# Attention into a wave-MLP on one core: three more sets of tiles turned by transposing transfers, and a rewritten order of all steps

## The chip, the core and the metric

The kernel runs on one core of a Trainium2 chip. The metric is the device time of one launch in microseconds (us). TensorE (PE) has its own queue for weight loads (PEld) beside that of the matmuls; VectorE (DVE), ScalarE (ACT), GpSimd (POOL) and SyncE (SP) each run their own instructions in program order and wait for one another through semaphores. All transfers of this kernel, in and out of the chip's memory or from one on-chip tile to another, are issued by SP, one after the other.

## The reference, cut to what matters

```python
# q, k, v: (8 batches, 8 heads, 576 rows, 64), float32; factor = 4
out_d   = softmax(mean4(q) @ mean4(k).T / 8) @ mean4(v)     # 144 rows, repeated 4 times
out_loc = softmax(where(|i-j| < 4, q @ k.T / 8, -1e9)) @ v  # a band of width 7
x = (repeat4(out_d) + out_loc)  as (8, 576, 512)
theta = x @ w_theta
y = w_tok_r @ (x * cos(theta)) + w_tok_i @ (x * sin(theta)) # over the 576 rows
u = x + y
return u + max(u @ w_ch, 0)                                 # (8, 576, 512) float32
```

## The kernel before, in words

Everything is one straight program over 8 batches, with no loop on the chip. Each piece of work is a *step*, a small Python function with a two-letter name, and the text `ORDER` (lines 57 to 98) names the steps one after the other. A step issues its instructions when its word is read, and `pin()` (line 696) ties each instruction to the one before it on its engine, so the text fixes the order of every engine's queue and of SP's. The letters behind a word choose the place: a PSUM bank or pair of banks for TensorE's steps, one of 14 staging tiles for loads, and `v`, `a` or `g` (VectorE, ScalarE, GpSimd) for copies and elementwise work that more than one engine can do. In the kernel before, the steps of one name come in a fixed sequence (batch by batch, line 709), and the word holds only the place.

The steps of one batch, in the order in which the data needs them:

- **Loads and casts.** `lk`, `lq` load two heads of k or q (line 288); `ck`, `cq` cast them to bf16 (line 297). `lv`, `lw` load the two halves of one of five row blocks of v (line 349), `cv` casts them (line 397). Batch 0 takes v another way (`l1`, `c1`, `t1`, `e1`, `x1`, lines 367 to 395).
- **Turning k and q.** `tp` turns two heads pairs on TensorE with 9 transposes (line 304) and `ev` copies the result out (line 317). For batch 7 a transposing transfer does it (`dk`, line 308).
- **Coarse attention.** `kd`, `qd` sum groups of 4 (lines 323, 331 to 337), `pv` and `vd` do it for v, `sd`, `ed`, `nd`, `xn`, `xd`, `xc` are scores, exponentials, weighted sums, normalization, a transpose and its copy.
- **Band attention.** `ps` (line 483) are scores of 116 rows at a time, `ex` exponentials, `mk` the multiplication with the band mask (line 502, on VectorE or GpSimd), `po` the weighted sums (line 512), `nm` the normalization on VectorE (lines 520, 521), `xt` and `xa` turn the result and add the coarse part (lines 531, 537). This gives `xT`, x with the 512 channels on partitions.
- **Wave.** `th` (line 548) is theta, `cs` its cosine and sine on ScalarE (lines 553, 554), `tt`, `ct`, `zt` the same for the last 64 rows. For `zz` (line 594, VectorE), which multiplies x by cosine and sine, x is needed with the rows on partitions: `xm` turns a quarter of it with 4 transposes on TensorE into a PSUM bank (line 587), or `dx` does it with a transposing transfer of SP into the tile `xx` (line 590). `xx` exists once and is shared by all batches that use it; four `dx` fill it, and each of the four `zz` needs all four.
- **Mixing.** `mx` is 9 matmuls (line 610), `ua` adds x on VectorE (line 615) and gives `uT`.
- **Last part.** `ch` is u @ w_ch (line 635). The residual u with rows on partitions, `ur`, comes from `up` (4 transposes on TensorE, line 624) and `uc` (a copy, line 627), or from `du`, a transposing transfer (line 619). `rl` (line 640, VectorE) makes the output tile, `st` stores it. `ut`, `dt`, `ht`, `rt`, `ss`, `sr` do the last 64 rows of two batches at a time.

`xm` serves batches 0 to 5 and `dx` batches 6 and 7; `up` serves batches 0 to 3 and `du` batches 4 to 7. The word `wm` issues matmuls on a tile of zeros whose result is not used (line 715); the text has 37 of them. `te` and `ts` load ScalarE's table for exponentials or for sines (line 720).

Of the kernel before, what the change touches and what calls it, by code (L numbers as in the profile page):

```python
# [8 lines left out]
FP32 = mybir.dt.float32  # L9
# [5 lines left out]
P = 128  # L15
# [14 lines left out]
NCH = 5  # L30
# [15 lines left out]
XDMA = (6, 7)  # L46

RPE = (0, 1, 2, 3)
# [9 lines left out]
l10 l11 c1g c1g k0 l12 lk3 l14 ckg c1v lk5 wm0b t101 c1g e1a kcg wm24 t123 e1a lq6 wm45 x12 cva ckg x13 cva x10 cvv  # L58
cqg lq7 lk8 lk9 tp45 cqg kcg kcg x12 lqa eva lqb kdg cvv kca cka wm62 tp67 lkc x13 lkd cvv eva ckv wm13 pv01 cqv lq0
la2 cqg lb1 tp45 qdv eva wm22 tp23 eva wm65 ps67 kdg vdv lq3 qdv ckg cka ps45 cag ex wm25 sd23 ex lb4 ed cbg lk5 sd01  # L60
cqg ps67 mkv ed po45 nm po23 nd45 nd01 la6 nm la7 xn xn lk8 mkg tp23 cag po45 ex xt6 po01 cqa eva la9 lqa mkg caa xd7
lqb ckg xca ckg nm tp23 nm xt4 xt5 lbd cag lbc cbg lb2 xt7 xa cqg lb1 eva lb0 cbg lb3 lb6 tp01 xa po23 th4 xa xm5 xa
lv7 cqg nm cbg th6 lw xt7 cbg th2 lv5 xm3 evv cbg ts cs tp01 lv8 lv9 cs cbg xa tt4 zz cs xm5 wp6 wp2 zz lw lw wp3 lw
lv4 lw cbg lqa zz ct lqd eva qdg ztv wp7 cba th4 wcv zp5 lkb xm6 wcv lkc kdg wcv wp2 wp3 wcv zcv wp0 wcv wp1 cs wp7
wca wcv ps45 lk2 lk1 wcv wcv ps23 te ex qdg ps01 lq0 zz kdv cva ex mx7 mx6 mx4 cvg ua sd23 cvg cvg mkv lc3 ex po01 ua
sd67 ed ed mkv mx5 ua nm po23 ua po01 cvg pv67 nm nm mkg vda mx4 ua po23 lq6 cqg po67 nd01 nm nd45 mx2 up3 xn lq7 ckg
xn cqg lk5 cka nm tp01 xd4 lk8 up5 uca eva xcv xt3 ucv lk9 tp67 cka xt4 xt0 ua ckg xt1 kdg lv4 xa xa xa mx5 xa eva lva
tp23 ua th4 xt0 lw xa evv cqg th5 xm1 lvb lcd lqc tt0 lw lk1 lv2 lv0 lw ts cs lw xm4 cqg cs tp67 ckg cqg th2 xm3 th5
ct lw cka zz tp01 cs qdg zz cs xm2 evv ztg lc6 lc5 zp4 mx6 ccg zz qdg zcv zz eva cvg mx7 ps45 te ex ua ps23 ua ckg kdv
ex mkv ps01 mx6 lq7 mx7 po45 sd23 ex lq8 lk3 kdg ed cvg sd01 cqg ckg ua lk4 lq9 mx6 tp23 mkv lva lw lvc lw nm ua tp45  # L70
up7 cvg mkv cvv ed mx0 eva cvg pv23 ccg ua ucv eva po67 po45 ua nm up1 nm vda ccg ccg ch0 nd67 lq1 xn nd23 lkb cqg cqa
tp45 uca qdg xn mx1 xd2 xt3 eva ps67 rl lq0 ua po45 xcv kdg qdg ps01 ch2 xa ckg ex mkg nm rl mx3 ps67 cqg lv2 cka po45
ex ua sd01 lkd xt2 ckg ex nm mx3 xt4 xt5 xa up2 ua cqa cqg tp67 cvv ed up3 xa evv uca th0 xa lv6 xt1 up2 xa lw th4 xm6
ucv ts cs uca th5 cvg lq5 ckg po01 cvg zz cs nm po23 xm7 cs ch6 nm tt4 tp01 lw ct tp23 th5 rl mkg ch4 lq7 zz st eva
evv rl po67 sd01 cs cqg cvg ztg po23 ch5 nm nm rl ch4 lv8 lw te ed cvg st pv67 vda zp0 zca lk4 cka lk3 lk1 tp23 cqa
mkg ckg lq9 lqb rl qdg lva lw xm1 eva ckg utg lv0 zz lw xm5 ch4 nd67 lvc zz xn lw nd01 mx5 lvd xn mx6 st ps23 rl lv2
ua po01 kdg nm ps45 ua mx7 lk5 ex xd0 cqa xt1 ex up6 ua xcv ucv lk6 kdv tp23 cqg utg mx0 tp45 qdg xa ua eva sd67 xt2
lv8 xt3 ch1 eva xa mkg ed xa th0 mkv rl cvg lk3 lw xt6 xt7 xa xa lw lk1 cvg th2 mx1 ua ts cs xm3 cvg tt0 zz th6 st lq4
cs cvg cka po45 dt cvg ckg ct po23 th7 mx1 ztg lk7 cs lvb nm pv45 cs ckg po67 cqg kdg lw nm ua sd23 mx0 cvg nm te ed
zp1 tp67 vdv zcv ht2 tp45 xm1 rt lw ua lq9 mx3 eva zz ps67 eva ua lva qdg po45 nm ex ps01 lq0 ex xm2 up3 zz lqc nd67  # L80
uca lvd tp45 cqa xm2 qdg xn nd01 zz mx3 cka cka xn mx2 xd0 up1 lk2 lv6 kdg st ua mx3 cqa mkv lw uca xcv eva tp67 xt0
up1 lk5 ua ua cva ucv xt4 xa mx5 st xa st eva ps23 mkg sd01 qdg po67 lw ed ua nm lv3 xt4 mx5 xt6 cva mx7 po01 ua ex
sd23 xa xa po45 lw nm cvg th6 nm lq4 cqv xt0 lw ed cvv xa ts cs tp23 mkv lv8 th1 cs xm4 ua ch5 kdg lw rl ch6 lv9 eva
tt0 th1 th7 xm5 pv23 utv ct ztg zz up0 ss cqg cs zz vdv mx1 uca ua xm0 lv1 lw st zz cs tp45 lv7 cvg lv0 cvg lqb nd23
xm7 ch1 eva kdg rl nd45 xn mx0 rl xn dz ch1 sr ps23 ps45 lw lw qdg lw te ex lka zz po67 ua mx0 ex ps23 cqa ex nm rl ua
lkd ps67 mkv po45 mx1 up0 mkg nm ckg sd23 po45 ua mkg lqc nm ex sd67 utg cka cvg lv6 uca mx1 ch0 cva xt4 ua st st xd1
xca cvg mx5 ed mx1 ed up2 lw xa ua rl xt3 ua uca pv45 cqg po67 xa lq4 nm po01 xt2 cvv th3 up6 vda ucv lq3 xt7 mx4 ch5
# [6 lines left out]
xa th0 zz xa ztg dz tt2 zz zz cs rl mx1 ch4 ct cs ch2 dx dx rl rl dx dx th5 ua mx4 ua cs zz mx2 ua ch4 mx0 zz zz mx1  # L94
ua ua mx2 st mx0 rt ztg cs dz st st ua du zz ua mx5 st ss du ua du mx1 rl ua mx0 ua mx1 mx0 ua ua du st du mx1 mx0 ua
mx1 du ua ua mx0 ch1 ua du rl ch0 ch5 ch1 ch4 rl ch0 ch3 sr du utv rl st st utg dt rl st ch1 rl rl st ht0 rl st rl rt
st st st ss sr
"""


@with_exitstack
def kernel(
# [414 lines left out]
    def nm(b, c, w):  # L517
        ps = at.pop(("po", b, c))
        r = rl[c % 2]
# [238 lines left out]
```

## Time and profile before

| | |
|---|---|
| runs timed | 3: 231.39, 231.49, 232.36 us; median 231.49 |
| profiled execution, first to last instruction | 229.4 us |
| busy: PE, PEld, DVE, ACT, POOL | 219.7, 154.2, 185.6, 159.3, 144.1 us |
| share of the 16 DMA engines | 83.4% |
| transposing transfers | 36 (8 `dx`, 16 `du`, 4 `dz`, 4 `dk`, 4 `dt`) |

The profile has no other time of the profiled execution than its span; the difference to the median of the runs, 2.1 us, is what lies before the first and behind the last instruction of the record. A matmul's busy time is from its start to its modelled end, and matmuls overlap, so a busy PE is not a full one: what one step costs the PE queue is read from the chain of work, where each step stands with the time until the next.

### The profile page before, as it was taken

How to read it: one execution, taken by the hardware profiler on the slowest of the kernel's cores; microseconds unless marked ns; L12 is line 12 of the kernel's file. 1: busy time of each engine (PE TensorE's matmuls, PEld its weight loads, DVE VectorE, ACT ScalarE, POOL GpSimd, SP SyncE). 2: the span in 40 equal slices, each digit the busy share in tenths (PEclk: the TensorE clock that was granted, in tenths of full speed). 3: DMA queues.
4: the chain of work that ended last, by engine and by line, in shares of the span. 5: the costliest groups of instructions: out<-in, count | busy, mean ns of one | idle time of the engine just before them, and what ended most of it. 6: DMA issues, size and time to landing. Idle time of an engine off the chain costs nothing.

```text
span 229.4 us, 8506 instructions
## 1 busy us (share of the span) xinstructions
PE 219.7 (96%) x3491; PEld 154.2 (67%) x3491; DVE 185.6 (81%) x377; ACT 159.3 (69%) x239; POOL 144.1 (63%) x190
## 2 busy tenths in 40 slices
PE   7898899999999999999999999899999999999992
PEld 2455778696778765776788667676676665677740
DVE  5168999999899899797898969979898889476382
ACT  2389899759987899689887896779879258600000
POOL 7768999929999989991984456892697310200000
PEclk9999999999999999999999999999999999999998
DMA  6999999999989999999998007996576357376677
GB/s 181 387 391 391 268 190 222 374 271 226 235 270 249 248 345 177 231 261 233 291 220 211 21 17 191 302 214 126 136 132 187 68 118 206 74 207 160 94 239 241
DMA packets 76647, 49.35 MB, mean 215 GB/s; under 512 B 61120, under 2 KB 61120, under 8 KB 76608
## 3 DMA queue, kind: packets, MB, share of 16 engines
q1 hardware_dynamic: 76608, 48.81, 83.4%
q8 instruction: 27, 0.44, 0.8%
q14 instruction: 12, 0.10, 0.1%
HBM read 33.98 MB, written 9.44 MB: 189 GB/s over the span
## 4 chain that ended last, share of the span: by engine, by line
PE 86%; DVE 7%; DMA 3%; issue 2%; SPq 1%; ACT 0%; POOL 0%; DVEq 0%
PE PS L610 30%; PE PS L548 12%; PE PS L635 12%; PE PS L304 5%; PE PS L531 4%; PE PS L512 3%; DMA st<-in_v_dram 3%; PE PS L587 2%; PE PS L483 2%; PE PS L448 2%; PE PS L560 2%; DVE tmp L521 2%; PE PS L624 2%; PE PS L652 2%; PE PS L453 1%
## 5 line engine op out<-in xcount | busy, mean ns | idle before, releaser
L610 PE MATMUL PS<-WT,z 128*128 128x288 bf16 x576 | 77.9, 286 | 0.2 <-issue 0.2
L610 PEld LDWEIGHTS <-z 128*128 128x128 bf16 x576 | 54.3, 98 | 15.8 <-issue 0.9
L615 DVE TENSOR_TENSOR uT<-PS,xT 128x288 bf16<-128x288 f32 x64 | 28.8, 452 | 11.8 <-PE PS L610 10.9
L548 PE MATMUL PS<-wth,xT 128*128 128x512 bf16 x128 | 32.2, 379 | 0.0
L635 PE MATMUL PS<-wch,uT 128*128 128x512 bf16 x128 | 31.1, 379 | 0.0
L569 POOL TENSOR_TENSOR zT<-xT,cst 128x512 bf16<-128x512 bf16 x7 | 8.1, 1153 | 34.0 <-ACT cst L566 34.0
L521 DVE TENSOR_TENSOR tmp<-PS,rl 128x512 bf16<-128x512 f32 x40 | 27.7, 692 | 1.4
L502 POOL TENSOR_TENSOR pm<-pm,band 128x1024 bf16<-128x1024 bf16 (+1 forms) x14 | 25.0, 1789 | 4.5 <-ACT pm L491 4.5
L537 DVE TENSOR_TENSOR xT<-PS,xdT 128x464 bf16<-128x464 f32 (+1 forms) x40 | 24.0, 629 | 3.0 <-ACT xdT L471 2.0
L640 DVE SCALAR_TENSOR_TENSOR osb<-PS,ur 128x512 f32<-128x512 f32 x32 | 21.8, 685 | 4.7 <-PE PS L635 4.2
L491 ACT ACTIVATE pm<-PS 128x1024 bf16<-128x1024 f32 (+1 forms) x24 | 20.4, 879 | 6.5 <-PE PS L483 6.5
L553 ACT ACTIVATE cs<-PS,pihc 128x512 bf16<-128x512 f32 x32 | 22.2, 693 | 1.6 <-PE PS L548 1.4
L720 ACT ACT_TABLE_LOAD x15 | 19.2, 1283 | 0.3
L331 POOL TENSOR_TENSOR two<-kT 128x580 f32<-128x580 bf16 x13 | 15.0, 1152 | 7.0 <-ACT kT L317 5.3
L635 PEld LDWEIGHTS <-uT 128*128 128x128 bf16 x128 | 11.9, 98 | 11.1
L554 ACT ACTIVATE cs<-PS 128x512 bf16<-128x512 f32 x32 | 19.2, 601 | 0.0
L594 DVE TENSOR_TENSOR z<-PS,cs 128x1024 bf16<-128x1024 bf16 x24 | 16.0, 682 | 2.3 <-PE PS L587 1.8
L548 PEld LDWEIGHTS <-xT 128*128 128x128 bf16 x128 | 11.3, 98 | 9.6 <-DVE xT L537 0.2
L331 POOL TENSOR_TENSOR two<-qT 128x576 f32<-128x576 bf16 x13 | 14.9, 1145 | 4.3 <-ACT qT L317 4.0
L438 ACT ACTIVATE pd<-PS 128x864 bf16<-128x864 f32 x16 | 13.8, 888 | 5.0 <-PE PS L427 4.9
L397 POOL CAST v_w<-st 128x512 bf16<-128x512 f32 x26 | 16.8, 672 | 0.0
L317 ACT COPY qT<-PS 128x1152 bf16<-128x1152 bf16 x13 | 14.6, 1121 | 2.0 <-PE PS L304 2.0
(116 smaller groups left out, 427.0 us busy)
## 6 DMA issues: line engine op xcount, KB each, us to landing
st<-in_k_dram SPq DMA_DIRECT2D x32, 288.0 KB, 6.0
st<-in_q_dram SPq DMA_DIRECT2D x32, 288.0 KB, 6.1
st<-in_v_dram SPq DMA_DIRECT2D x70, 128.0 KB, 5.2
out_dram<-osb SPq DMA_DIRECT2D x32, 256.0 KB, 2.4
st<-in_v_dram SPq DMA_DIRECT2D x4, 288.0 KB, 3.2
st<-in_moe_w_tok_r_dram SPq DMA_DIRECT2D x4, 288.0 KB, 6.5
st<-in_moe_w_tok_i_dram SPq DMA_DIRECT2D x4, 288.0 KB, 7.4
st<-in_moe_w_theta_dram SPq DMA_DIRECT2D x4, 256.0 KB, 6.3
```

Source lines behind the costliest of these rows:

```text
L331: nc.gpsimd.tensor_tensor(out=t, in0=src[:, :, 0:2], in1=src[:, :, 2:4], op=ALU.add)
L491: nc.scalar.activation(out=pm[(3 * b + u) % NPM][:, :, 0:n].rearrange("p e c j w -> p e (c j w)"), in_=at.pop(("ps", b, u))[:, :, 0:4 * W ...
L502: EW[w].tensor_tensor(out=t, in0=t, in1=m, op=ALU.mult)
L521: nc.vector.tensor_tensor(out=tmp[(NCH * b + c) % NTMP].rearrange("p g (j d) -> p g j d", d=D), in0=ps[:, :, :, 0:D], in1=r.unsqueeze(3).t ...
L537: nc.vector.tensor_tensor(out=xT[b % 2][:, :, CH * c:CH * c + cnt].rearrange("p e (m j) -> p e m j", j=4), in0=at.pop(("xt", b, c))[:, :, ...
L548: nc.tensor.matmul(out=ps, lhsT=xT[b % 2][:, dc, P * c:P * c + P], rhs=wth[:, dc, :], start=(dc == 0), stop=(dc == 3))
L553: nc.scalar.activation(out=t[:, 0, :], in_=ps, func=AF.Sin, bias=pihc, scale=1.0)
L554: nc.scalar.activation(out=t[:, 1, :], in_=ps, func=AF.Sin, bias=0.0, scale=1.0)
L610: nc.tensor.matmul(out=ps, lhsT=z[b % 2][:, j, P * dc:P * dc + P], rhs=WT[:, j, cols], start=(j == 0), stop=(j == 8))
L615: nc.vector.tensor_tensor(out=uT[b % 2][:, dc, cols], in0=at.pop(("mx", b, i)), in1=xT[b % 2][:, dc, cols], op=ALU.add)
L635: nc.tensor.matmul(out=ps, lhsT=uT[b % 2][:, dc, P * c:P * c + P], rhs=wch[:, dc, :], start=(dc == 0), stop=(dc == 3))
L640: nc.vector.scalar_tensor_tensor(out=o, in0=at.pop(("ch", b, c)), scalar=0.0, in1=ur[b % 2][:, c, :], op0=ALU.max, op1=ALU.add)
```

## The change

The two constants that choose the way of `x` and of the residual change, the scratch tile of `nm` gets five copies in place of two, each word of the order now names its step in full (name, batch, part, then the place behind a dot), so that steps of one name may come in any sequence, and the whole text of the order is new, with other places and engines.

```diff
-XDMA = (6, 7)
+XDMA = (4, 5, 6, 7)
-RPE = (0, 1, 2, 3)
+RPE = (0, 1, 2)
 ORDER = """
-l10 l11 c1g c1g k0 l12 lk3 l14 ckg c1v lk5 wm0b t101 c1g e1a kcg wm24 t123 e1a lq6 wm45 x12 cva ckg x13 cva x10 cvv
-cqg lq7 lk8 lk9 tp45 cqg kcg kcg x12 lqa eva lqb kdg cvv kca cka wm62 tp67 lkc x13 lkd cvv eva ckv wm13 pv01 cqv lq0
...
-mx1 du ua ua mx0 ch1 ua du rl ch0 ch5 ch1 ch4 rl ch0 ch3 sr du utv rl st st utg dt rl st ch1 rl rl st ht0 rl st rl rt
-st st st ss sr
+l100.0 c100.g kc1.a kc2.g l103.1 c103.a l102.2 c102.a wm.27 t101.01 e101.v kc0.a l101.3 lq01.4 lq00.5 cq00.v c101.g
+wm.42 t100.23 e100.a cq01.g wm.42 tp001.01 lk03.6 ck03.g lq03.7 lq02.8 kc3.a lk02.9 cq02.g ck02.g x104.2 cq03.v cv04.v
...
+xt71.4 du53 nm72.v th60.5 vd7.a nd70.23 th62.6 cs62.a xn70.v dx61 nd71.01 xn71.v st43 xt73.2 th63.3 xt72.6 xd7.7 st31
...
+ua74.v du72 mx72.2 ua73.v ua72.v du71 mx71.0 ch61.1 ua71.v ut7.v mx70.0 ch63.4 dt3 rl61.v st61 ua70.v ch62.5 du70
+rl63.v st63 rl62.v st62 ch60.0 rl60.v ch72.4 rl72.v ht3.5 rt3.v sr2 st60 st72 ss3 sr3 ch70.0 rl70.v st70 ch73.4 ch71.5
+rl73.v st73 rl71.v st71
 """
-    rl = tiles(2, [P, 2, 4], "rl", FP32)
+    rl = tiles(NCH, [P, 2, 4], "rl", FP32)
-        r = rl[c % 2]
+        r = rl[c]
-    todo = {kind: iter(seq) for kind, (_, seq) in STEPS.items()}
+    todo = {(kind,) + tuple(args) for kind, (_, seq) in STEPS.items() for args in seq}
     for word in ORDER.split():
-        kind, place = word[:2], word[2:]
+        word, _, place = word.partition(".")
+        kind, args = word[:2], tuple(int(x) for x in word[2:])
...
-        STEPS[kind][0](*next(todo[kind]), place)
+        todo.remove((kind,) + args)
+        STEPS[kind][0](*args, place)
```

The new text has 20 `wm` matmuls in place of 37, 16 `dx` in place of 8 and 20 `du` in place of 16, 16 `xm` in place of 24 and 12 `up` in place of 16. Steps that several engines can do, as VectorE / ScalarE / GpSimd:

| step | before | after |
|---|---|---|
| casts of k and q (`ck`, `cq`) | 3 / 20 / 41 | 9 / 11 / 44 |
| v blocks (`cv`) | 7 / 7 / 26 | 8 / 13 / 19 |
| w_tok (`cb`) and their turned copies (`wc`) | 8 / 2 / 8 | 10 / 4 / 4 |
| w_theta, w_ch (`ca`, `cc`) | 0 / 1 / 7 | 1 / 1 / 6 |
| `ev` and `e1` | 5 / 27 / 2 | 7 / 25 / 2 |
| sums of four (`kd`, `qd`) | 6 / 0 / 26 | 6 / 0 / 26 |
| masks (`mk`) | 10 / 0 / 14 | 11 / 0 / 13 |
| `uc`, `xc`, `vd`, `zc` | 17 / 19 / 0 | 13 / 19 / 0 |
| `zt`, `ut` | 5 / 0 / 11 | 7 / 0 / 9 |
| mask tiles and v of batch 0 (`kc`, `c1`) | 1 / 1 / 6 | 0 / 5 / 3 |

The other steps of VectorE (`nm`, `xn`, `xa`, `zz`, `ua`, `rl`, `rt`) and of ScalarE (`ex`, `ed`, `cs`, `ct`, the table loads) are as many as before.

108 lines of the change are left out of this document (69 added, 39 removed).

## The prediction

> **What bounds the kernel now.** I read the page first, then the chain of waits, then engine busy time by stage, then rows by line and form, last the timeline.
>
> ```profile
> span 229.4 us, 8506 instructions
> PE 219.7 (96%) x3491; PEld 154.2 (67%) x3491; DVE 185.6 (81%) x377; ACT 159.3 (69%) x239; POOL 144.1 (63%) x190
> PE 86%; DVE 7%; DMA 3%; issue 2%; SPq 1%; ACT 0%; POOL 0%; DVEq 0%
> ```
> ```profile
> by line: PE PS L610 30.4%; PE PS L548 12.2%; PE PS L635 12.2%; PE PS L304 5.3%; PE PS L531 3.7%; PE PS L512 3.0%; DMA st<-in_v_dram 2.6%; PE PS L587 2.5%; PE PS L483 2.3%; PE PS L448 1.7%; PE PS L560 1.6%; DVE tmp L521 1.6%; PE PS L624 1.6%
> ```
>
> The end is set by TensorE: 86% of the chain is its matmuls, one behind the other. So matmul work taken out anywhere behind the start comes off the time nearly whole, as long as no other queue then arrives late. Which could, and where, the stages show (columns: length; busy time of PE, PEld, DVE, ACT, POOL; clock; DMA share; GB/s).
>
> ```profile
> 0.00:28.80 28.80, 24.80 (x403) 15.14 (x404) 19.08 (x51) 18.72 (x24) 23.36 (x50) 1.00 0.97 324
> 124.00:136.00 12.00, 12.00 (x205) 7.74 (x204) 9.43 (x22) 9.95 (x16) 5.40 (x7) 1.00 0.22 48
> 160.00:180.00 20.00, 20.00 (x371) 14.40 (x369) 17.75 (x36) 16.24 (x24) 15.74 (x14) 1.00 0.60 136
> 180.00:200.00 20.00, 20.00 (x213) 12.12 (x210) 15.70 (x32) 12.46 (x24) 2.31 (x2) 1.00 0.55 132
> ```
>
> In the head, up to 28.8 us, GpSimd is the fullest of the four engines beside TensorE, whose figure there holds overlap and warming matmuls. Later TensorE is full, VectorE 79 to 89% busy.
>
> The profiled execution spans 229.4 us, the median of the runs is 231.5; I carry the 2.1 us between them unchanged and make the sum on the span.
>
> **Part by part: matmuls removed.** Eight `xm` (32 transposes) and four `up` (16) go.
>
> ```profile
> L587 PE MATMUL PS<-ident,xT 128*128 128x128 bf16 x96 | 9.1, 219 | 0.0
> L624 PE MATMUL PS<-ident,uT 128*128 128x128 bf16 x64 | 6.2, 219 | 0.0
> 65.92 1.00 PE PS L304 x18
> 38.36 3.41 PE PS L610 x27
> ```
>
> The 219 ns is a latency; the chain row has 18 transposes of the same shape in 1.00 us, 56 ns each. By that 48 cost 2.7 us. By the chain's shares it is 2.5% of 229.4 for 96 and 1.6% for 64: 60 and 57 ns, 2.8 us. I take 2.7, all on the chain. The four `uc` copies also go, from ScalarE or VectorE, and cost nothing now.
>
> **The waits between VectorE and GpSimd.** Where one mask step meets another, the trace shows a stall that ends up on TensorE (columns: start, length).
>
> ```profile
> 144.73 1.73 DVE L502 TENSOR_TENSOR pm<-pm,band 128x512 bf16<-128x512 bf16 x1
> ```
> ```profile
> 144.05 2.12 POOL L502 TENSOR_TENSOR pm<-pm,band 128x1024 bf16<-128x1024 bf16 x1 [2.60 <-ACT pm L491]
> ```
> ```profile
> 147.36 0.32 PE L512 MATMUL PS<-v_w,pm 64*64 64x65 bf16 x16 [0.94 <-DVE tmp L521]
> ```
> ```profile
> L502 DVE TENSOR_TENSOR pm<-pm,band 128x1024 bf16<-128x1024 bf16 x7 | 5.7, 814 | 0.0
> L502 DVE TENSOR_TENSOR pm<-pm,band 128x512 bf16<-128x512 bf16 x3 | 4.2, 1387 | 0.0
> ```
>
> VectorE's mask of half the size takes 1.73 us and ends 0.3 us after GpSimd's mask ends: it waited for that. The group rows say the same: 512 elements cost 1387 ns and 1024 cost 814. Half of 814 is 407, so three steps lost about 2.9 us, and TensorE idled 0.94 us behind one of them. The new order moves these steps; it may lose 0 to 2 such stalls or gain some. I take a gain of 0.9, this one stall, with ends +1.9 and -1.
>
> **Engines.** By the counts of the change and these rows
>
> ```profile
> L397 POOL CAST v_w<-st 128x512 bf16<-128x512 f32 x26 | 16.8, 672 | 0.0
> L262 POOL CAST uT<-st 128x576 bf16<-128x576 f32 x8 | 5.1, 662 | 0.0
> L317 DVE COPY kT<-PS 128x1152 bf16<-128x1152 bf16 x4 | 5.4, 1347 | 0.0
> ```
>
> GpSimd loses 7 casts of v (4.7 us), 4 of w_tok (2.6), a mask of 2.1 and smaller steps: about 11 us less. VectorE gets 2 more copies of k or q (2.7), 6 casts of k and q at an estimated 0.6 and others, and loses four small copies: about 5 more. ScalarE comes out even. VectorE would be busy some 191 of 226 us, 84% after 81%. I cost that at nothing in the middle, where 11 to 21% of its time is idle; without that cover it would cost up to the 5 us.
>
> **The head.**
>
> ```profile
> 28.83 0.99 PE PS L548 x4
> ```
> ```profile
> 5.86 1.00 DVE L373 CAST z<-st 128x512 bf16<-128x512 f32 x2 [1.06 <-DMA st<-in_v_dram]
> ```
> ```profile
> 0.00:5.30 5.30, 4.04 (x10) 1.50 (x11) 3.23 (x21) 1.28 (x1) 3.94 (x20) 1.00 0.65 177
> 5.30:28.80 23.50, 20.75 (x394) 13.64 (x393) 15.85 (x30) 17.44 (x23) 19.42 (x31) 1.00 1.04 357
> ```
>
> Up to the first theta step the new order gives GpSimd about 3 us less work, but VectorE about 7 more (a 1.35 us copy of v, a 1.35 us sum, two masks, casts, three more `xa`), and TensorE 2 us of work that the old order does later. VectorE's first data come at 5.9; its 15.9 us from there to 28.8 become 22.9, the whole time. So theta starts no earlier: at 28.8 if VectorE never stands, at 30.7 if it is 92% dense, at 32.8 with 85%. Against that 2.0 us of matmuls are then done already. The head lies between 2.0 better and 2.0 worse; I take the middle case, 92%, which is even: 0. The 17 `wm` matmuls that go fill time in which TensorE waits anyway, and cost nothing either way.
>
> **SyncE's queue.** Twelve transposing transfers come on top, all issued in order with loads and stores.
>
> ```profile
> L590 SPq DMA_TRANSPOSE xx<-xT x8: 1189/1264/2213, 179.1 to 199.6; - x8
> ```
> ```profile
> L619 SPq DMA_TRANSPOSE ur<-uT x16: 1189/1240/1832, 154.1 to 217.7; - x16
> ```
> ```profile
> 105.61 0.61 SPq L349 DMA_DIRECT2D st<-in_v_dram  x1
> 164.82 0.53 SPq L644 DMA_DIRECT2D out_dram<-osb  x1
> 135.93 1.23 SPq L573 DMA_TRANSPOSE z<-zT  x1
> ```
> ```profile
> 151.16 1.38 SPq L308 DMA_TRANSPOSE st<-q_tm  x1
> ```
> ```profile
> 225.66 1.12 SPq L661 DMA_DIRECT2D out_dram<-osb  x2
> ```
> ```profile
> SPq L573 <- POOL v_w L397: 13.1, 1, 13.1
> ```
>
> 12 x 1.25 is 15 us more issue time. Before, the queue stood 13.1 us for the first `dz` (batch 4), so there is room. From that `dz` to the last store the old queue holds 31 transposes of 1.25, 4 `dk` of some 1.6, 31 stores of 0.53, 11 halves of v at 0.61 and 5 loads of about 0.5: 71 us of issue in 226.8 - 135.9 = 90.9. The new one holds 37, 4, 31, 10 and 8: 80 us. And there the `dz` stands with 73 us of matmuls behind it instead of 79, so that the stretch is about 84 us long. 4 us of slack are left of 20. Who waits: a `dx` delays `zz` on VectorE, which holds up the `ua` queued behind it, and so TensorE's banks.
>
> ```profile
> DVE z L594 <- DMA xx<-xT: 1.2, 1, 1.2
> ```
>
> Two batches on `dx` cost 1.2 us of such waiting; two more give an estimated 1.2, and a fuller queue adds. On TensorE I take +0.5, with ends 0 and +5.
>
> **zz on two on-chip operands.**
>
> ```profile
> L594 DVE TENSOR_TENSOR z<-PS,cs x24: 674/680/692, 32.4 to 166.7; 128x1024 bf16<-128x1024 bf16 x24
> L594 DVE TENSOR_TENSOR z<-xx,cs x8: 682/682/692, 191.7 to 206.5; 128x1024 bf16<-128x1024 bf16 x8
> ```
>
> For batches 4 and 5 `zz` will read `xx` in place of PSUM. Alone that is no slower (682 against 680 ns); but all eight old cases ran after 191 us, where GpSimd was nearly done (2.3 us busy from 180 to 200). In 160 to 180 it was 79% busy. The mask step reads two such operands and showed waits: at its 1024 elements a mean of 814, 0.13 over `zz`, at 512 up to 1.0 of wait. Eight `zz` wait 1.0 to 8 us on VectorE; I take the mean of the same size, 1.0, of which 0.2 reach TensorE. The Trainium skill, SBUF — State Buffer, section Who interferes with whom, says that a VectorE instruction with two SBUF inputs contends with a GpSimd one that reads SBUF, the later one waiting for the whole of the earlier. The trace agrees where two masks met; no `zz` of this trace shows it.
>
> **The end.** Both orders close with the last `ch` matmuls, one VectorE step and a store; the new one ends with one store instead of two of 0.56 each, but SyncE is fuller: 0. The five `rl` scratch tiles are written and read by VectorE alone, in order: 0.
>
> Sum: -2.7 - 0.9 + 0 + 0.5 + 0.2 = -2.9: span 226.5, time 228.6 us.
>
> **The rivals.**
>
> *The head becomes VectorE's and the old stall only moves.* GpSimd's load falls, but the fullest engine is only exchanged. For: 22.9 us of work in 22.9. Against: GpSimd, the fullest before with 19.4 of 23.5, gets 3 us less to do, and its sums are what the scores wait for. Head +2.0 with VectorE at 85%, no gain on stalls: -2.7 + 2.0 + 0.7 = 0, 231.5 us: no change.
>
> *`zz` meets GpSimd.* Eight waits of up to 1.0 put 8 us on VectorE in some 40 us, where it had 11 to 20% idle (2.3 of 20 us from 160 to 180). Some 3 us stay uncovered: 231.6 us, no change. For: the mask's rows. Against: the 814 row, and GpSimd has 11 us less to do. This is what the page's rule would do if every `zz` met a GpSimd step.
>
> *SyncE becomes the bound, and the kernel slower.* Place: from the `dz` of batch 4 to the end. With 80 us of issue in 84, it decides as soon as the queue stands idle for more than 4 us there, waiting in order for an `xT`, `zT` or a cast. The old queue stood for about 20 us in that stretch. If the new one stands 10, the stretch is 80 + 10 = 90 in place of 84 us: 6 us over the forecast, 234.6 us. For: the queue is strictly in order, and its loads of batch 7 lie between transposes. Against: the order can put ready transfers ahead, and the old idle time was partly lead.
>
> *More is gained.* Head 2.0, two stalls 1.9, no cost at `dx`: -2.7 - 2.0 - 1.9 = -6.6, 224.9 us. For: nothing but the ends of the bounds.
>
> That the transfers do not replace the matmuls can be excluded from the diff.
>
> **How the numbers follow.** About 0.5%, 1.2 us, is what a measurement of this kernel can tell from no change. Forecast 0.52 (225.5 to 230.3), more gained 0.13, VectorE's head 0.12, `zz` 0.08, SyncE 0.15. Faster: 0.52 + 0.13 = 0.65. Slower: SyncE's 0.15 and the upper part of the head and `zz` cases, 0.03: 0.18. Same: the rest of those two, 0.17. The forecast's own range is 225.5 to 230.3. The range that leaves out about 2 in 10 goes from 224.6, with part of the better case below it, to 232.4, with most of SyncE's case above it.
>
> **What would show it.** L587 with 64 matmuls and L624 with 48, so 2.7 us of them gone; the first theta near 29 to 31 us with more matmuls ahead of it; `zz<-xx` x16 with a mean near 0.75 us; few VectorE masks over 1 us; SyncE's idle time behind batch 4's `dz` near 4 us, its last store issued within 1 us of the last `rl`. I am wrong if TensorE idles over 1 us at a time behind `zz`, if `zz<-xx` takes over 1 us on average, or if SyncE is never idle in the last 80 us while stores are ready.

## The result, and the profile after

The changed kernel takes 241.9 us (median of 4 runs) against 231.4: a ratio of 1.042, 95% interval 1.034 to 1.049. It is slower, by 4%, where I forecast 228.6 us. One of the four runs, of 244.4 us, was in a slower state of the chip and is not in the ratio; the other three have a median of 240.9. Its profiled execution spans 238.3 us (240.0 with what lies around it).

The page of the changed kernel: span, busy time, and the shares of the chain of work by engine.

```profile
span 238.3 us, 8314 instructions
PE 216.4 (91%) x3399; PEld 151.3 (64%) x3426; DVE 191.1 (80%) x388; ACT 158.7 (67%) x246; POOL 136.3 (57%) x173
PE 56%; DVE 16%; DMA 11%; ACT 7%; SPq 4%; issue 4%; DVEq 0%; ACTq 0%
```

TensorE had 86% of the chain and has 56%; what it lost went to VectorE, to transfers and to the queue. The counts are as forecast (rows of TensorE, then of VectorE by form):

```profile
L619 PE MATMUL PS<-ident,xT 128*128 128x128 bf16 x64 | 5.7, 219 | 0.0
L656 PE MATMUL PS<-ident,uT 128*128 128x128 bf16 x48 | 4.6, 219 | 0.0
```
```profile
L626 DVE TENSOR_TENSOR z<-xx,cs 128x1024 bf16<-128x1024 bf16 x16 | 10.8, 717 | 0.0
L534 DVE TENSOR_TENSOR pm<-pm,band 128x1024 bf16<-128x1024 bf16 x9 | 7.9, 883 | 0.3 <-ACT pm L523 0.2
L534 DVE TENSOR_TENSOR pm<-pm,band 128x512 bf16<-128x512 bf16 x2 | 0.8, 408 | 0.0
```

Now the stages from 160 to 200 us, as in the prediction (length; busy time of PE, PEld, DVE, ACT, POOL; clock; DMA share; GB/s). TensorE was full there; now it stands for 1.1 and 2.8 us, and its granted clock drops.

```profile
160.00:180.00 20.00, 18.91 (x241) 13.30 (x242) 15.03 (x30) 11.32 (x13) 10.13 (x9) 1.00 1.03 178
180.00:200.00 20.00, 17.22 (x230) 10.37 (x234) 15.03 (x33) 9.97 (x19) 5.50 (x5) 0.91 0.76 160
```

To see where the time goes when the order itself is new, I lay each kernel along its own work: every matmul step counts with the time that it costs on TensorE in the chain of the kernel before (an `mx` 1.10 us, a `th` 0.86), the steps that turn x and the residual count nothing, and the sum is made in each kernel's own sequence. The table gives the time in which a profiled execution does that stretch of the same work.

```
us of TensorE's work  before  after | left out  sorted  by need  by need, tiles in turn
  0 to  20             39.3   39.4  |   40.3     39.5     40.7     39.5
 20 to 100             85.4   88.9  |   89.1     88.7     88.3     89.3
100 to 140             44.0   41.2  |   41.3     42.5     41.3     41.3
140 to 150             10.7   15.1  |   10.5     14.6     10.5     11.0
150 to 190             40.0   41.1  |   45.5     40.2     41.8     41.4
190 to the end         10.0   12.6  |   10.5     12.3     12.3     11.0
span                  229.4  238.3  |  237.2    237.8    234.9    233.5
```

(The four columns on the right are experiments below.) The saved transposes are there to be seen: -2.8 us between 100 and 140, where `xm` of 4 and 5 and `up` of 3 stood. Against that stand +3.5 between 20 and 100, +4.4 in one place between 140 and 150, +1.1, and +2.6 at the end: 8.9 in all, with +0.1 in the head. Where a stretch begins depends on the cost put on each step. With the median cost of each kind of step the changed kernel loses 0.9 up to 20 us and 2.1 from there to 100, together 3.0 in place of 3.6; the later stretches move by 0.6 at most.

The one place is near 180 us. The chain of work there (start, length):

```profile
175.18 0.63 SPq L381
...
175.86 0.62 SPq L676
...
176.53 5.25 DMA utr<-ut
...
181.91 0.70 DVE osb L688
...
182.65 0.32 PE PS L544 x16
182.97 2.05 PE PS L642 x9
```

SyncE issues half loads of v (L381) and a store (L676), then the turned residual of pair 1 (`dt`), whose source had been ready at 153.6. VectorE's output step waits for it, VectorE's mask stands behind that, and TensorE's `po` behind the mask:

```profile
DVE osb L688 <- DMA utr<-ut: 3.7, 1, 3.7
PE PS L544 <- DVE osb L688: 2.2, 1, 2.2
```

The nine matmuls after it took 2.05 us instead of 1.10. At the end the waits are of another kind: VectorE for the store of the output tile that it is to fill.

```profile
DVE osb L688 <- DMA out_dram<-osb: 2.4, 1, 2.4
PEld L667 <- issue: 2.0, 1, 2.0
PE PS L667 <- DVE osb L688: 1.8, 1, 1.8
```

And SyncE's queue: from 134.2 us to its last store it never stands for 1 us. Waits of the queue, from 134 us on:

```profile
SPq L651 <- DVE uT L647: 3.0, 4, 0.9
```

The longest single wait of the queue is 0.9 us in that row, where in the kernel before one alone was 13.1.

### The profile page after: what moved, and what is told of

It is laid out like the page before. It is cut to its first block, busy times and chain, and to the rows that moved or that the text cites. A ratio compares the mean times of both kernels' runs of the same rounds, so it can differ in the third digit from the quotient of the medians.

```text
span 238.3 us, 8314 instructions
## 1 busy us (share of the span) xinstructions
PE 216.4 (91%) x3399; PEld 151.3 (64%) x3426; DVE 191.1 (80%) x388; ACT 158.7 (67%) x246; POOL 136.3 (57%) x173
## 4 chain that ended last, share of the span: by engine, by line
PE 56%; DVE 16%; DMA 11%; ACT 7%; SPq 4%; issue 4%; DVEq 0%; ACTq 0%
PE PS L642 21%; PE PS L667 9%; PE PS L580 7%; DVE xT L569 3%; PE PS L544 3%; DMA st<-in_q_dram 2%; DMA out_dram<-osb 2%; PE PS L336 2%; PE PS L563 2%; DMA utr<-ut 2%; DVE z L626 2%; DMA st<-in_v_dram 2%; ACT kT L349 2%; DVE uT L294 2%; DMA xx<-xT 2%
## 5 line engine op out<-in xcount | busy, mean ns | idle before, releaser
L642 PE MATMUL PS<-WT,z 128*128 128x288 bf16 x576 | 79.1, 288 | 0.2
L647 DVE TENSOR_TENSOR uT<-PS,xT 128x288 bf16<-128x288 f32 x64 | 28.0, 450 | 10.2 <-PE PS L642 9.5
L580 PE MATMUL PS<-wth,xT 128*128 128x512 bf16 x117 | 30.6, 379 | 1.1 <-DVE uT L647 0.3
L569 DVE TENSOR_TENSOR xT<-PS,xdT 128x464 bf16<-128x464 f32 (+1 forms) x40 | 23.4, 628 | 2.4 <-PE PS L563 1.4
L534 POOL TENSOR_TENSOR pm<-pm,band 128x1024 bf16<-128x1024 bf16 (+1 forms) x13 | 23.0, 1777 | 1.9 <-ACT pm L523 1.6
L363 POOL TENSOR_TENSOR two<-qT 128x576 f32<-128x576 bf16 x14 | 16.9, 1208 | 8.0 <-DVE qT L349 6.2
L329 POOL CAST k_tm<-st 128x576 bf16<-128x576 f32 x22 | 15.3, 699 | 7.4 <-PE PS L336 3.1
L601 POOL TENSOR_TENSOR zT<-xT,cst 128x512 bf16<-128x512 bf16 x6 | 6.9, 1154 | 21.9 <-ACT cst L598 21.9
L329 POOL CAST q_tm<-st 128x576 bf16<-128x576 f32 x22 | 14.9, 690 | 3.5 <-DMA st<-in_q_dram 3.4
L429 POOL CAST v_w<-st 128x512 bf16<-128x512 f32 x19 | 12.2, 648 | 5.0 <-DMA st<-in_v_dram 4.9
```

The source lines that it names most:

```text
L329: COPY[w](out=to[:, r, :], in_=of[:, r, :])
L363: nc.gpsimd.tensor_tensor(out=t, in0=src[:, :, 0:2], in1=src[:, :, 2:4], op=ALU.add)
L534: EW[w].tensor_tensor(out=t, in0=t, in1=m, op=ALU.mult)
L569: nc.vector.tensor_tensor(out=xT[b % 2][:, :, CH * c:CH * c + cnt].rearrange("p e (m j) -> p e m j", j=4), in0=at.pop(("xt", b, c))[:, :, ...
L580: nc.tensor.matmul(out=ps, lhsT=xT[b % 2][:, dc, P * c:P * c + P], rhs=wth[:, dc, :], start=(dc == 0), stop=(dc == 3))
L642: nc.tensor.matmul(out=ps, lhsT=z[b % 2][:, j, P * dc:P * dc + P], rhs=WT[:, j, cols], start=(j == 0), stop=(j == 8))
```

## The experiments

The first theory, **S**: the 12 transfers fill SyncE's queue, what it issues comes late, and that costs the 80 us at the end. The rivals: **O**, the new order of the other engines is slow by itself; **H**, the head gives away what it gains.

**The transfers taken back, and put in alone.** One kernel keeps the new order but turns x of 4 and 5 and the residual of 3 on TensorE again (each turning step on a free bank, some 14 words ahead of its reader); the other keeps the old order and puts each transfer right behind the word that fills its source.

```diff
-XDMA = (4, 5, 6, 7)
-RPE = (0, 1, 2)
+XDMA = (6, 7)
+RPE = (0, 1, 2, 3)
```

> The changed kernel's order, banks and engines, but x of batches 4 and 5 and the residual of batch 3 go through TensorE again as before (XDMA back to (6, 7), batch 3 back among the residuals of TensorE), 12 transposing transfers fewer on SyncE's queue. Theory S (SyncE's queue is full from 110 us on, and late transfers cost the last 80 us): 12 x 1.25 = 15 us of issue less; SyncE's queue idles over 18 us after 110 us (7 in the changed kernel, about 20 before), the 23-us lateness of batch pair 1's residual transfer goes, the run gains 6 to 8 of the lost 9.5 us and pays 48 x 0.056 = 2.7 us of transposes again: 234 to 238 us. Rival O (the new order itself is slow, the transfers are not): 241 plus 2.7, about 243 us, with the same loss between 150 and 200 us.

248.3 us, ratio 1.070 (1.064 to 1.077): slower still, which neither theory said. The steps that I put in wait for their banks (TensorE's waits from 136 to 160 us),

```profile
PE PS L619 <- DVE kT L349: 1.6, 1, 1.6
PE PS L642 <- DVE z L626: 1.2, 1, 1.2
PE PS L619 <- DVE xdn L491: 1.0, 1, 1.0
```

and the queue, with nothing ahead of them, stood 13.6 us for batch 4's `dz` and 11.4 for a `dk`, with batch 7's loads behind. The kernel has waits of its own making and tells S and O not apart.

> The order, banks and engines of the kernel before, with only the 12 transposing transfers put in: x of 4 and 5 and the residual of 3 leave TensorE, each transfer issued right after the row tile that it reads. Theory S: SyncE gets the same 15 us more of issue, so its idle 20 us after 110 us shrink to about 5, and late issues cost what they cost in the changed kernel from 150 us on, less the 2.7 us of transposes: 233 to 240 us. Theory H (a good part of the loss is the head's, where the new order lets VectorE's casts meet GpSimd, and the rest is the new order's placing of late words): 228.7 to 232 us, first chunk product at 38.4 us as before. Rival O likewise says 229 to 232.

249.4 us, ratio 1.078 (1.074 to 1.082). The head is the old one (first chunk product at the old time), so none of this kernel's loss is H's. It is far over the 233 to 240 of S. The queue's waits show the cause:

```profile
SPq L645 <- DVE uT L641: 14.9, 1, 14.9
```

The first `du` of batch 3 stood 14.9 us in the queue for its source, with loads behind it. At that point SyncE had been issuing some 15 us ahead of TensorE; that lead was lost, and it was then some 9 us behind.

**The head.** Five casts of the token weight go from VectorE to GpSimd (`cb7.v` to `cb7.g` and four more).

> The changed kernel with the five casts of the token weight that VectorE makes (1028 ns each there, since GpSimd works beside them) put on GpSimd, behind its other three. Theory H: TensorE reaches the first chunk product 1.5 to 3 us before the 40.0 us of the changed kernel, and if nothing later sets the pace anew, the time falls by as much, to 238 to 239.5. Theory S: the head's gain is eaten by SyncE's queue later, which is paced by its own 1.25-us issues: 240 to 241.5, no change. If the casts in a row on GpSimd are later than on both engines, the first chunk product comes at 41 to 43 us, and the time is 241 to 243.

241.3 us, ratio 1.041 (1.035 to 1.046), unchanged; the first chunk product came at 41.0 instead of 40.0, as the third case says. The head was made later, not earlier, and the time did not follow. That speaks against H but does not test it; by the table the head costs 0.1 us, with the median costs 0.9.

**Stores where they are ready.** Every store and `dt` goes right behind the word that fills its tile (`rl11.v ... st11` becomes `rl11.v st11`).

> The changed kernel with only SyncE's order of late words changed: each output store and each transposing transfer of the residual pair is put right behind the word that fills its tile, instead of up to 20 us of queue later. Same transfers, same order on all other engines. Theory S1 (the place in the queue does the harm): the 3.7-us wait of VectorE for the turned residual pair 1 goes, and the waits of output tiles for their stores: 235.5 to 238. Theory S2 (the amount of issue work does it): the loads and turned tiles behind them come later by as much: 239.5 to 243, SyncE idle after 110 us still about 7 us.

311.8 us, ratio 1.347 (1.341 to 1.353), far outside both. SyncE's waits:

```profile
SPq L676 <- DVE osb L672: 69.5, 21, 11.1
```

A word of the order is no point in time: SyncE reads some 10 us ahead here, so "right behind the producer" makes it stand up to 11.1 us, 21 times, with loads behind. A late store is a smaller evil than a waiting one.

**The transfers left out.**

```diff
-mx33.6 lk60.2 du30 cv53.g
+mx33.6 lk60.2 cv53.g
...
+        nc.vector.memset(xx, 0.0)
...
-dx=(dx, [(b, c) for b, c in span(B, 4) if b in XDMA])
+dx=(dx, [(b, c) for b, c in span(B, 4) if b in XDMA[2:]])
-du=(du, [(b, c) for b, c in span(B, 4) if b not in RPE])
+du=(du, [(b, c) for b, c in span(B, 4) if b not in RPE and b != 3])
```

> The changed kernel without its 12 new transposing transfers: the eight of x and the four of the residual are left out, and their readers read what the tiles held before (one tile is filled with zeros at the start). All other instructions, their order, banks and engines are the changed kernel's. Theory S (the 15 us that the 12 transfers take of SyncE's queue, back to back from 134 us on, make the loss): TensorE is at 150 us of its work 4 to 6 us earlier than in the changed kernel, SyncE idles 15 us or more after 110 us, and the time is 231 to 235: the new order's own 3.6 us, which the changed kernel has lost by 100 us of TensorE's work, less the 2.7 us of transposes, on 231.8. Rival O (the new order itself, transfers or not): 239 to 241.5.

239.0 us, ratio 1.035 (1.030 to 1.040): only some 2 us come back, and the interval overlaps the changed kernel's. By the table the place at 140 to 150 is healed, but 150 to 190 takes 5.5 us more than before. S in its first form is wrong: the queue got 15 us of room and used it for waiting,

```profile
SPq L605 <- POOL two L363: 10.9, 1, 10.9
SPq L340 <- POOL q_tm L329: 6.8, 1, 6.8
```

while everything behind those two words issued as late as with the transfers. Behind 130 us of work 69.9 us of issue were left, against 72.5 in the changed kernel and 58.0 in the kernel before. The chain near 200 us:

```profile
194.55 2.49 DMA xx<-xT
...
205.51 4.56 DMA xx<-xT
...
211.32 0.60 DVE z L626
211.92 0.61 DVE osb L672
212.57 1.02 PE PS L684 x4
```

**Stores from ScalarE.** `nc.sync.dma_start` becomes `nc.scalar.dma_start` in the 40 output stores.

> The changed kernel with its 40 output stores issued from ScalarE's queue instead of SyncE's: about 0.5 us each, 20 us less on SyncE, the 12 new transfers stay. Theory S by amount of issue (the queue is full, whatever fills it): SyncE idles over 15 us after 110 us, the late residual turn of pair 1 comes earlier, 233 to 237. If the transfers themselves are what costs (their bytes, their tiles), 239.5 to 242. If ScalarE, which must now wait for each output tile, becomes late for its sines and exponentials: over 242.

250.2 us, ratio 1.081 (1.076 to 1.085). By the number it is the third case, but that sines and exponentials are late is not shown: of VectorE's waits those for a store grow, to 15.0 us in all from 2.4. This says nothing for or against S.

**Eight transfers by time, old order.** x of 4 and the residual of 3, each where the queue of the kernel before stood when the source was ready:

```diff
-lq70 ... dz4 sr0 lw63 lw64 lw70 lk72 ... st20
+du30 lq70 lw63 lw64 lw70 du31 dx40 dx41 dx42 dx43 ... du32 dz4 sr0 lk72 ... du33 st20
```

> The order, banks and engines of the kernel before, with eight of the 12 transfers: x of batch 4 and the residual of batch 3. Each is put into SyncE's queue where that queue of the kernel before stood when its source was ready (most of them into the 12 us for which it waited for batch 4's last chunk of z), three half loads of v are put ahead of them, and the four multiplications of batch 4 stand behind on VectorE. Theory S (a transfer is free where the queue idles and dear where it does not): 32 transposes of 0.056 us less on TensorE, 1.8 us, and no loss: 229 to 231 us against 231.8. If a transposing transfer costs whatever its place: 233 to 238, as with the same transfers put right behind their sources (249).

234.7 us, ratio 1.017 (1.014 to 1.020). Some 15 us better than the transfers behind their sources (12 there, 8 here), but slower than the kernel before, and by the number what the rival said. The loss is one stall:

```profile
PE PS L662 <- DVE osb L667: 3.9, 1, 3.9
```

It is not the queue's. I had put the four `zz` of batch 4 in a row ahead of the output step that frees TensorE's bank, and beside GpSimd they took far longer than 680 ns, 4.8 us together in place of 2.7. So 2.1 us of the stall are their length, and the rest is their place (min/median/max ns, 130 to 150 us):

```profile
L621 DVE TENSOR_TENSOR z<-xx,cs x4: 1116/1151/1630, 137.3 to 141.0; 128x1024 bf16<-128x1024 bf16 x4
```

**One late transfer earlier.** `dt1` goes from behind `st23` to ahead of `dk700`.

> The changed kernel with one word of SyncE's queue moved: the transposing transfer of residual pair 1, ready at 153.6 us and issued at 176.5, goes ahead of batch 7's four turned k and q loads (the first of which issued at 160.1). Theory S by place: VectorE's 3.7-us wait for that tile and TensorE's 2.2 us behind it go, the jump of 5.5 us of TensorE between 178 and 187 us shrinks to 2 to 4, and the time is 238 to 240. Theory S by amount: what stood behind comes 1.25 us later and the time stays, 240 to 242.

241.2 us, ratio 1.046 (1.041 to 1.050): no change, as S by amount says, but not for its reason. The wait for that tile is gone, and another chain ends at the same `po`: a half load of v, behind it on GpSimd its cast, two sums, and the mask.

```profile
174.99 2.77 DMA st<-in_v_dram
...
177.88 0.61 POOL v_w L429
178.49 1.12 POOL two L363
...
182.31 1.12 POOL pm L534
...
183.48 0.32 PE PS L544 x16
```

That stall is down to 0.9 us, from 1.1 and 2.2 in two pieces, but near 150 us TensorE stood for two others, 1.5 and 1.8, that the changed kernel does not have. So the stall did shrink here, and what it gave went to those two. The first stands behind two `zz` of 2.6 us together. The transfer of batch 4's x landed a little later there, and its last two `zz` met GpSimd's mask (VectorE's row, then GpSimd's):

```profile
147.90 3.21 DVE L626 TENSOR_TENSOR z<-xx,cs 128x1024 bf16<-128x1024 bf16 x2
```
```profile
148.22 2.34 POOL L534 TENSOR_TENSOR pm<-pm,band 128x1024 bf16<-128x1024 bf16 x1 [1.55 <-ACT pm L523]
```

**The queue sorted by readiness.** So place, not number? **S2**: what is ready stands behind what is not.

> The changed kernel with all its instructions and transfers, and the order of every engine but SyncE unchanged. From 95 us on SyncE's queue is sorted anew, by the time at which each transfer's source or target was ready in the changed kernel's trace (stores 1.5 us, batch 7's v loads 6 us, the residuals of 3 and 4 5 us behind that), so that nothing that is ready stands behind something that is not. Theory S2 (not the number of transfers but their place: at the same point of TensorE's work, 130 us, 72.5 us of issue are still to come in the changed kernel, 69.9 with the 12 transfers left out, 58.0 in the kernel before, because transfers not yet ready held the queue up to then): with the same durations the sorted queue would hold few transfers later than 8 us, against up to 51, and would be idle again for about 9 us after 180; the time falls to 232 to 236. Theory O (the order of the other engines sets the time, the queue is only full beside it): 239 to 242.

263.0 us, ratio 1.137 (1.131 to 1.142), for a fault of mine: sorted words had jumped ahead of seven that the changed kernel issues before 95 us. Mended:

```diff
-st11 dt0 st03 lq61 lv51 lw51 lv50 lw50 lq63 st10 lv64 lq60 st13 lv63 lk63 lv54 ...
+lq61 st11 lv51 lw51 lv50 lw50 lq63 lv64 lw64 lq60 lv63 lw63 lk63 dt0 st12 lv54 ...
```

> The sorted queue once more, mended: in the first sorted kernel the words sorted from 95 us on had also jumped ahead of seven loads and stores that the changed kernel issues before 95 us, and those loads came 20 us late, so that it tested nothing. Now all words up to those stay where they were, and only what the changed kernel issues after 95 us is sorted by readiness. Same transfers, all other engines' order as in the changed kernel. Theory S2 (place in the queue): few transfers over 8 us late, SyncE idle again after 180 us, 232 to 236. Theory O (the other engines' order sets the time): 239 to 242. Over 243: a queue sorted by readiness in one trace makes its own delays, and place is not so simple.

240.6 us, ratio 1.042 (1.036 to 1.048): no change, although SyncE now stood 3.2 us near 200 and 65.2 us of issue were left behind 130. The stall at 140 to 150 is still there (14.6), with a third releaser: a turned q load of batch 7, issued at 170 though ready at 161, and GpSimd's copies behind it.

```profile
173.97 4.26 POOL qT L346 x2
178.23 0.56 POOL v_w L429
178.79 1.12 POOL two L363
...
182.90 1.16 POOL pm L534
...
184.09 0.32 PE PS L544 x16
```

**More issues in the kernel before.** The other way round: no transposing transfer more, but each of 24 late stores in two halves of 64 rows.

```diff
+        n = P // 2 if b >= 2 else P
+        for r in range(0, P, n):
+            nc.sync.dma_start(out=out[b, P * c + r:P * c + r + n, :], in_=o[r:r + n])
```

> The kernel before with each of the 24 output stores of batches 2 to 7 issued as two of 64 rows, nothing else: 24 more issues of about 0.55 us, 13 us, on SyncE's queue, all of them late, no transposing transfer more and the same bytes. Theory S2: of the 11.3 us that the queue has free behind 130 us of TensorE's work some 3 are left in every kernel, so about 8 of the 13 us are hidden and 5 come out at the end: 235 to 238. Theory O: the queue has room, and stores are waited for by nobody but the output tiles: 231 to 232.5.

242.0 us, ratio 1.048 (1.044 to 1.053), against 231.1 for the kernel before beside it: 13 us of issue cost 10.9, more than either theory said, and with the old order untouched. Of the 10.8 us by which its span grew, 7.7 lie behind 190 us of work, where output tiles wait for stores (218 us to the end):

```profile
DVE osb L640 <- DMA out_dram<-osb: 3.7, 3, 1.8
PE PS L655 <- DVE osb L640: 1.5, 1, 1.5
```

From 137 us on the queue stands for 4.1 us in all, where it stood for 13.2. So a full queue does cost the end, whatever fills it.

**By need.** Three runs had ended at the same stall with three releasers. **S3**: several chains of late transfers end there, and one alone relieved shows nothing (with `dt1` earlier the stall had shrunk, so only the sorted queue shows this cleanly). The queue is now ordered so that of the ready transfers the one with the nearest reader goes first; nothing else changes.

```diff
-dx50 du33 dx53 dx52 dk700 dz5 dk711 dk701 st22 st20 dk710 st21 lv72 du40 lw72 lv74 ...
+du33 st20 dx51 dx50 dx53 dx52 dz5 dk700 dk701 st22 lv72 dk710 dk711 lw72 lv74 lw74 dt1 ...
```

> The changed kernel once more with only SyncE's queue reordered from 95 us on, now by need: among the transfers that are ready, in the times of the sorted kernel's trace, the one whose first reader comes soonest goes first. Against the sorted kernel the last two turned k and q loads of batch 7 issue 5 to 8 us earlier (163 instead of 170), and with the changed kernel's residual pair 1 early too, both chains that end at TensorE's stall near 180 us are relieved at once. Theory S3 (two chains of late transfers end at the same TensorE instruction, so relieving one alone showed nothing): the 4.4 us lost between 140 and 150 us of TensorE's work go, 235.5 to 238. Theory O (the other engines' order sets the time): 239 to 242 with the stall still there under another releaser.

238.7 us, ratio 1.036 (1.028 to 1.043), runs of 236.6 to 240.4; the profiled one, the fastest of them, spans 234.9. That is just above S3's range, and the interval overlaps the changed kernel's, so the gain of the whole run is not clear of noise. The stall is gone (10.5), and from 140 to 190 us of work TensorE's longest wait is

```profile
PE PS L667 <- DVE xT L569: 1.0, 1, 1.0
```

> The changed kernel with the 12 new transfers left out (their readers read old contents) and SyncE's queue by need as well. Theory S3: without the transfers and with no word waiting in vain, the 5.5 us that the kernel with the transfers left out loses between 150 and 190 us of TensorE's work go too; what is left is the other engines' order, 3.6 us lost by 100 us of work, less 2.7 us of transposes: 232 to 235. Theory O: 237 to 239.5 as with the transfers left out alone (239.0).

236.5 us, ratio 1.024 (1.020 to 1.029), against 239.0 without the new sequence, and the intervals are apart: place alone is worth 2.5 us with no new transfer involved. It lies between the two forecasts. Between this kernel and the last lie the 12 transfers: 2.2 us by the medians, and their intervals overlap. The rest, 5.5 us over the kernel before, is neither the new transfers nor the late sequence of the queue. O would explain it, but so would, in part, the choice of output tile, and the sequence of SyncE's loads ahead of 95 us, which is new too.

**Output tiles.** The changed kernel frees the sequence of its steps, but the five output tiles are still chosen by batch and part. By the order's text 14 of 31 reuses come 2 to 4 fills later, with only 1 to 3 other tiles filled between; before, 4 did, all with 3 between. In turn it is always 4.

```diff
-        o = at["o", b, c] = osb[(4 * b + c + b // 2) % NOSB]
+        o = at["o", b, c] = osb[turn[0] % NOSB]
+        turn[0] += 1
```

> The kernel with SyncE's queue by need, and beside it the five output tiles handed out in the sequence in which VectorE fills them, where the changed kernel chooses them by batch and part: with its steps in free sequence 14 of the 31 reuses come after 2, 3 or 4 other tiles, in the kernel before 4 (all after 4). Theory T (the 2.3 us lost behind 190 us of TensorE's work are waits of VectorE for the store of the tile that it is to fill): the waits of the last output steps for a store, 2.6 us, go, the stretch from there to the end takes 10.0 to 10.8 us in place of 12.3, and the time is 236 to 237.5 against 238.7. If the late stores of the full queue are the cause whatever the tile: 238 to 239.5.

235.5 us, ratio 1.018 (1.012 to 1.025): the interval lies below the changed kernel's and below that of the queue by need alone. The time is a little under T's range, the stretch a little over: behind 190 us of work it falls from 12.3 to 11.0, and of VectorE's waits for stores there stays

```profile
DVE osb L692 <- DMA out_dram<-osb: 0.4, 1, 0.4
```

> The changed kernel with nothing but the output tiles handed out in the sequence in which they are filled. Theory T: the wait of VectorE for a store at the end (2.4 us) and that of TensorE behind it (1.8) shrink, but SyncE's queue is still full and in the changed kernel's order, so the stores are late as before: 239 to 241 against 240.9 in the changed kernel. If tiles were the larger part of the loss: 236 to 238.

244.4 us, ratio 1.054 (1.044 to 1.064), worse than forecast by either. In this kernel some tiles are filled again before their store is issued (the changed queue has a store up to 51 us behind its tile), so part of the output is a later tile's. It shows that tile and place in the queue belong together, no more.

**Transfers in a queue with room.** Is a transfer free where there is room? Into the kernel before, with batch 3's residual by hand, then in order of need, then with batch 2's too:

```diff
-RPE = (0, 1, 2, 3)
+RPE = (0, 1, 2)
-... lq70 ... dz4 ... st20
+... du30 lq70 ... du31 du32 dz4 ... du33 st20
```

> The kernel before with the residual of batch 3 alone turned by four transposing transfers, three of them put into the 12 us that SyncE waits for batch 4's last chunk of z, the fourth right behind its source: 16 transposes of 0.056 us, 0.9 us, less on TensorE, four copies less on the other engines, and no change to the multiplications of z. If a transfer in an idle queue is free: 230 to 231.3 against 231.4. If every transposing transfer costs 0.4 us or more wherever it stands: 232 to 234.

> The same without batch 2's residual: the kernel before with batch 3's residual turned by four transfers, SyncE's queue from 100 us on in order of need. 0.9 us of transposes less: 229.8 to 231; as the same transfers placed by hand gave 230.8, a difference to that is what the order of need adds.

> The kernel before with the residuals of batches 2 and 3 turned by eight transposing transfers, x of 4 and 5 left on TensorE, and SyncE's queue from 100 us on in order of need by the times of the kernel with batch 3's residual alone; every other engine's order is the kernel before's. 32 transposes of 0.056 us less on TensorE, 1.8 us; by those times each of the eight would issue over 10 us ahead of its need. If a transfer is free wherever the queue has slack: 229 to 230.3 against 231.2. If the transfers' traffic delays loads that TensorE then waits for: 231 to 234.

230.8 (ratio 0.998, 0.995 to 1.000), 230.5 (0.9965, 0.994 to 0.999) and 230.9 us (0.997, 0.994 to 1.000), 12 runs each; the first and the third interval just include no change. Four cost nothing that shows: 0.9 us of transposes bring 0.3 to 0.7. Eight save twice as much and bring no more. There TensorE waits for the last chunk of z of batches 4 and 5, which it does not with four:

```profile
PE PS L636 <- DMA z<-zT: 2.5, 2, 1.6
```

The first of these two `dz` had its source at 135.0 and issued at 140.0, behind a turned residual, some loads and a store; the two landed 4.3 and 4.5 us after their issue, against 2.4 to 2.6 with four. So the rival, transfers that make others late, is seen with eight, and a transfer is free only as long as there is room. What lengthens the landing stays open. The second of the three is the one version that beats both kernels, by 0.35%, less than the half per cent that I called measurable.

## Why the prediction was wrong

- **Transposes, -2.7:** right, -2.8 between 100 and 140 us of work.
- **The stall of VectorE's half mask, -0.9:** right as a mechanism. The two such masks now take 408 ns each, where three took 1387. The gain is not in the time, though: between 100 and 140 us of work, where that stall lay, TensorE idles 0.9 us before and 1.1 after.
- **The head, 0:** nearly right by the sum (0.1, or 0.9 with the median costs), not by its working. VectorE got 4.0 us more work between 5.3 and 28.8 us (19.83 against 15.85), not 7, so the first theta came at 27.8, not 29 to 31; yet the first chunk product came at 40.0 instead of 38.4.
- **Engines, "at nothing in the middle":** the first term that failed. The engines' sums were fair (VectorE 191.1 us busy, as forecast; GpSimd 7.8 less, not 11). But between 20 and 100 us of work the changed kernel needs 88.9 us instead of 85.4, and so do the four kernels of the table with its order (88.3 to 89.3). TensorE idles 0.24 us in that stretch before and 1.8 after; VectorE is busy 76.5 of 85.4 us, then 77.5 of 88.9:

```profile
39.30:124.70 85.40, 85.16 (x1560) 63.62 (x1561) 76.51 (x149) 72.23 (x109) 69.36 (x87) 1.00 1.02 257
```
```profile
39.40:128.30 88.90, 87.11 (x1581) 64.57 (x1593) 77.49 (x154) 75.38 (x118) 65.77 (x78) 1.00 0.78 226
```

  That VectorE has 11 to 21% of room did not make the order free. Which of its many small waits makes the 3.5 us stays open: none is over 0.75 us, and I tried no kernel that mixes the two orders. One rival to the engines' order is untested too: the loads of this stretch have a new sequence in SyncE's queue as well, and GpSimd waits for them in the changed kernel, which it does not before:

```profile
POOL q_tm L329 <- DMA st<-in_q_dram: 2.1, 2, 1.5
POOL k_tm L329 <- DMA st<-in_k_dram: 1.3, 1, 1.3
```

- **SyncE's queue, +0.5:** the step that failed most (5.5 between 140 and 190 us of work). Its rival with 6 us, given 0.15, had the right place. I counted issue time against the length of the stretch and found 4 us of slack. The count was fair: the changed kernel's queue is full from 134 us on. What I left out is that in a full queue the sequence decides who is late. `dt` of pair 1 came 23 us late; it and batch 7's loads met at one `po` and cost 4.4 us. From 140 to 190 us of work the kernel before takes 50.7 us, the changed one 56.2, the same 12 transfers in another sequence 52.3, and the old sequence without them 56.0. My mechanism for that rival, a queue that stands idle for 10 us, was not the right one either: the changed kernel's never stood for 1 us. With the transfers left out it stood 17.7 us in two waits, and the kernel was still slow. That the queue was never idle while stores were ready is the one of my signs of being wrong that came.
- **`zz` on two on-chip operands, +0.2:** right for this trace (717 against some 680 ns, 0.6 us in all on VectorE). That it can be 2 us at once is seen in other kernels' traces.
- **The end, 0:** failed, +2.6. I compared the last steps and their stores, and did not ask which tile each fills. About 1.3 of it is the choice of tile (12.3 to 11.0), shown with the queue by need. The tile costs only where stores come late: with the transfers left out and the old choice of tile the stretch took 10.5. The rest I did not take apart.

Together: -2.8 for the transposes, +0.1 in the head, +3.5 from 20 to 100 us of work, +5.5 from 140 to 190 and +2.6 at the end make +8.9 on the span, where I had -2.9. With the sequence by need and the tiles in turn the change stands at 1.018, and what is left by the spans, 4.1 us, is as much as it has lost by 100 us of work (128.8 against 124.7). That the order of the other engines keeps it slower is argued, not shown.

## What to carry to other kernels

As long as an in-order queue has room, a transfer costs little by its number and much by its place (here four were free and eight were not): put it where the queue stands when its source gets ready, not behind the word that makes the source, and look who is behind it. When one late item is relieved and nothing changes, look at the same instruction in the new trace for a second releaser, and at the rest of the trace for new waits, before you call the first harmless. When steps get a free sequence, look for what is still indexed by the old one, such as the tiles of a ring.

## What the runs showed of the hardware

**`zz` beside GpSimd.** With both operands on chip a `zz` takes some 680 ns where GpSimd is nearly done (682 in the kernel before, behind 191 us); beside GpSimd's sums four in a row took 1116 to 1630, and one that met a 2.34-us mask 2610 (min/median/max, the kernel with `dt1` earlier):

```profile
L626 DVE TENSOR_TENSOR z<-xx,cs x16: 678/683/2610, 143.5 to 213.1; 128x1024 bf16<-128x1024 bf16 x16
```

The Trainium skill, SBUF — State Buffer, section Who interferes with whom, calls the port pair that VectorE and GpSimd share an exclusive lock; these traces agree: the longest `zz` starts 0.3 us behind the mask and ends 0.55 us after it, within the 0.68 that it takes alone. The rival that I gave 0.08 is real; in the changed kernel's own trace it hardly met.

**A stall costs twice.** In the changed kernel TensorE stood for 1.15 us (179.02 to 180.16), did 0.26 us of work, and stood for 2.23 more (to 182.65). The granted clock (the column after POOL) was 0.65 in the 4 us from 182:

```profile
178.00:182.00 4.00, 1.27 (x49) 0.84 (x47) 0.30 (x2) 2.96 (x4) 3.06 (x4) 1.00 1.41 147
182.00:186.00 4.00, 3.13 (x30) 2.14 (x31) 3.34 (x9) 0.00 (x0) 3.14 (x2) 0.65 1.01 281
```

After 3.9 us in one piece (the kernel with eight transfers by time) it was 0.50 in the next 4 us; after 1.5 and 0.9 us (the sorted kernel) it stayed 1.00. The Trainium skill, TensorE: Matmul & The Clock Gate, section What's actually happening, has the clock fall to half after an idle window of about 3.4 us. The one long stall and the two short ones agree; in the changed kernel 3.4 us of standing had a short piece of work in it, and the clock still fell.
